# Transposes of the identity in four places of TensorE's queue, and 128 rows instead of 113 in the first product

## The chip, the core and the metric

The kernel runs on one core of a Trainium2 chip. Its engines are TensorE (PE, with its weight loads shown apart as PEld), VectorE (DVE), ScalarE (ACT), GpSimd (POOL) and SyncE (SP, which issues most DMAs). The metric is the device time of one execution in microseconds (us).

## The reference

An agent attention (49 agents between 12480 queries and keys of 128 channels) feeds two expert layers, one after the other:

```
scale = 1 / sqrt(128)
sm(a, b) = softmax(scale * a @ b.T)        # row maximum taken off, 1e-9 added to the sum
agent_v  = sm(agents, k) @ v               # 49 x 128
x   = sm(q, agents) @ agent_v              # 12480 x 128
y   = (s * relu(x @ w_in)**2 + b) @ w_out  # 128 -> 2048 -> 128
out = relu(y @ w_in2)**2 @ w_out2          # 128 -> 2048 -> 128
```

Everything comes in and goes out as float32; the weights come as 64-bit floats and are decoded on the chip.

## The kernel before

**Stage 1, to about 84 us: the agents' values.** The keys come in 13 groups of up to 1024 rows. For each group `k_transpose` transposes eight blocks on PE (L401), `k_scores` multiplies them with the agents (L411), ACT copies the scores to `S` (L413), and `k_max` keeps a running maximum on DVE (L417). Then the maximum over all keys goes through PE twice: `mxk` is transposed (`ps_mt`, L442), DVE reduces it and spreads it on a diagonal (`mt`, `dm`), and a product with ones gives it to every partition (`ps_mb`, L450, copied to `mb`). After that `shift(g)` takes `mb` off a group's scores, on DVE for group 0 and on POOL for groups 1 to 12 (L477), and ACT takes the exponential (L478). PE sums the products with the values, 13 groups into one bank `ps_av` (L494; each product is two records in the trace). `colsum` adds eight products into `ps_cs` (L460), four ahead of the transpose of the normalized values `avn` (`ps_avT`, L510) and four behind it. Block 0 of the queries passes through the same queues: `q_transpose(0)` and `(1)` (L141) around `ps_mt`, `q_scores(0)` (`ps_s`, L167) behind `ps_mb`, `q_exp(0)` (L200), `q_norm(0)` (L206 to L214), `q_stack(0)` (`ps_x`, L223).

**The decode of the weights** is woven in: `fill(n)` issues n steps of it, some eight DVE operations per piece of 512 columns (L269 to L285), with a copy on ACT at its end (L287) and one at its start (L267).

**M = agent_v @ w_in** comes in four pieces (`m_piece`, L338): two at the end of stage 1 and two in the first steps of stage 2. `av` holds the agents' values twice, in columns 0 to 48 and 64 to 112, so that a product gives 113 rows (KS): the second copy meets the low halves of the probabilities in `X`. Rows between the two copies are zero.

**Stage 2, 28 blocks of up to 448 queries**, each in 8 steps. A step issues on PE four products `ps_h` of layer 1 (`up1`, L543, M as weights and X moving), six of layer 2 (`up2`, L554) and twelve of the two way-down products (`down`, L565), while ACT and DVE make the squared relu and its two halves (L530, L531, L112, L113). The remaining decode runs in the first steps.

**Order.** The program is written under a manual schedule: every engine takes its instructions in the order of the Python code, PE, DVE, ACT and POOL each from its own queue. Tiles come from pools: `ps_h` has two buffers of two PSUM banks each, which hold the transposed keys in stage 1 and the hidden layer in stage 2.

Of the kernel before, what the change touches and what calls it, by code (L numbers as in the profile page):

```python
# [9 lines left out]
F32 = mybir.dt.float32  # L10
F32R = mybir.dt.float32r
# [5 lines left out]
P = 128  # L17
# [21 lines left out]
def tile_agent_attention_two_moe(  # L39
# [14 lines left out]
    nc = tc.nc  # L54
    _, N, C = q.shape
    NA = agents.shape[1]
    DFF = w_in.shape[1]
# [4 lines left out]
    KS = GAP + NA  # L62
# [23 lines left out]
    const = ctx.enter_context(tc.tile_pool(name="const", bufs=1))  # L86
    qp = ctx.enter_context(tc.tile_pool(name="qp", bufs=2))
    ps_h = ctx.enter_context(tc.tile_pool(name="ps_h", bufs=2, space=bass.MemoryType.PSUM))
# [3 lines left out]
    ident = const.tile([P, P], F32, name="ident")  # L92
    ones = const.tile([P, P], F32, name="ones")
    aT = const.tile([P, GAP], F32, name="aT")
    M = [const.tile([KS, DFF], F32R, name=f"M{x}") for x in "hl"]
    av = [const.tile([P, KS], F32R, name=f"av{x}") for x in "hl"]
    s_sb = const.tile([P, 1], F32, name="s_sb")
    b_sb = const.tile([P, 1], F32, name="b_sb")
    ones_r = const.tile([P, P], F32R, name="ones_r")
# [5 lines left out]
    sTs = [const.tile([KS, 256], F32, name=f"sT{i}") for i in range(2)]  # L105
    aS = const.tile([P, KS], F32R, name="aS")
    halves = (0, slice(0, NA)), (1, slice(GAP, KS))
    Xs = [const.tile([KS, 512], F32R, name=f"X{i}") for i in range(2)]

    def split(dst, src, eng_lo, copy=nc.vector.tensor_copy):  # L110

        copy(dst[0], src)  # L112
        eng_lo.tensor_tensor(out=dst[1], in0=src, in1=dst[0].bitcast(F32), op=ALU.subtract)  # L113


    q_raw, qT, q_sT, q_e, q_st, X = {}, {}, {}, {}, {}, {}
# [17 lines left out]
    def q_transpose(t):  # L134
        _, p, j = blocks[t]
        n = p * j
        raw = q_raw.pop(t)
        if t < DIRECT:
            ps = ps_m.tile([P, 512], F32, tag="m", name="ps_q")
            for i in range(j):  # L140
                nc.tensor.transpose(  # L141
                    out=ps[:, i * p:(i + 1) * p], in_=raw[:p, i * C:(i + 1) * C], identity=ident[:p, :p]
                )
            qT[t] = qp.tile([P, 512], F32, tag="qh", name="qT")
            nc.scalar.copy(qT[t][:, :n], ps[:, :n])
        else:
            hi = qp.tile([P, 512], F32R, tag="qh", name="qh")
            lo = qp.tile([P, 512], F32R, tag="ql", name="ql")
            split((hi[:, :n], lo[:, :n]), raw[:, :n], nc.vector, nc.scalar.copy)
            qT[t] = (hi, lo)  # L150
# [9 lines left out]
    def q_scores(t):  # L160

        _, p, j = blocks[t]
        x = qT.pop(t)
        ps = ps_m.tile([P, 512], F32, tag="m", name="ps_s")
        sc = ps[:p, :j * NA].rearrange("p (j n) -> p j n", n=NA)
        for i in range(j):
            nc.tensor.matmul(out=sc[:, i], lhsT=x[:, i * p:(i + 1) * p], rhs=aT[:, :NA], start=True, stop=True)  # L167
        q_shift(t, sc)
# [28 lines left out]
    def q_exp(t):  # L197
        _, p, j = blocks[t]
        e = q_e[t]
        nc.scalar.activation(e[:p, :j], e[:p, :j], AF.Exp, scale=SCALE)  # L200
# [57 lines left out]
    def w_decode(raw, hi, lo, early):  # L258

        L, H = raw[:, :, 0], raw[:, :, 1]  # L260
        x = dec_p.tile([P, WC], I32, tag="x", name="x")
        li = dec_p.tile([P, WC], I32, tag="li", name="li")
        ex = dec_p.tile([P, WC], I32, tag="ex", name="ex")
        ts, stt = nc.vector.tensor_scalar, nc.vector.scalar_tensor_tensor
        xf = x.bitcast(F32)
        if early:
            nc.scalar.activation(xf, H.bitcast(F32), AF.Abs)  # L267
        else:
            nc.vector.tensor_single_scalar(out=x, in_=H, scalar=0x7FFFFFFF, op=ALU.bitwise_and)  # L269
            yield  # L270
        ts(out=li, in0=H, scalar1=0x1FF, scalar2=15, op0=ALU.bitwise_and, op1=ALU.logical_shift_left)
        yield
        ts(out=xf, in0=xf, scalar1=W_MIN, scalar2=W_MAX, op0=ALU.max, op1=ALU.min)  # L273
        yield
        stt(out=li, in0=L, scalar=17, in1=li, op0=ALU.logical_shift_right, op1=ALU.bitwise_or)  # L275
        yield
        ts(out=x, in0=x, scalar1=4, scalar2=1, op0=ALU.logical_shift_left, op1=ALU.logical_shift_right)
        yield
        stt(out=x, in0=H, scalar=-(2**31), in1=x, op0=ALU.bitwise_and, op1=ALU.bitwise_or)  # L279
        yield  # L280
        ts(out=ex, in0=x, scalar1=2**30, scalar2=-(2**23), op0=ALU.bitwise_xor, op1=ALU.bitwise_and)  # L281
        yield
        ts(out=x, in0=x, scalar1=2**30, scalar2=-(2**12), op0=ALU.bitwise_xor, op1=ALU.bitwise_and)
        yield
        stt(out=lo, in0=li, scalar=2.0**-35, in1=ex.bitcast(F32), op0=ALU.mult, op1=ALU.mult)  # L285
        yield
        nc.scalar.copy(hi, xf)  # L287
# [12 lines left out]
    def next_load():  # L300
        if to_load:
            src, i, pair = to_load.pop(0)
            loaded.append((w_load(src, i), i, pair))

    def fill(n):

        for _ in range(n):
            if len(running) < 2 and loaded and (not running or min(x[1] for x in running) >= 4):
                raw, i, pair = loaded.pop(0)
                left = len(to_load) + len(loaded) + len(running)  # L310
                sl = slice(i * WC, (i + 1) * WC)
                running.append([w_decode(raw, pair[0][:, sl], pair[1][:, sl], left >= NW), 0])
            if not running:
                return
            r = running.pop(0)
            r[1] += 1
            try:
                next(r[0])
                running.append(r)
            except StopIteration:  # L320
                done.append(0)
            for i in range(len(done)):
                done[i] += 1
            if done and done[0] > 3:
                done.pop(0)
                next_load()
# [6 lines left out]
    def m_piece(i):  # L333

        sl = slice(i * WC, (i + 1) * WC)
        ps = ps_m.tile([P, 512], F32, tag="m", name="ps_M")
        for z, (x, w) in enumerate(((av[0], wi[1]), (av[1], wi[0]), (av[0], wi[0]))):
            nc.tensor.matmul(out=ps[:KS], lhsT=x, rhs=w[:, sl], start=(z == 0), stop=(z == 2))  # L338
        split((M[0][:, sl], M[1][:, sl]), ps[:KS], nc.vector, nc.scalar.copy)

    with tc.manual_schedule():

        with tc.tile_pool(name="pre", bufs=1) as pre, tc.tile_pool(name="kp", bufs=2) as kp:
# [42 lines left out]
            ps = ps_m.tile([P, 512], F32, tag="m", name="ps_w")  # L386
            for i in range(16):
                nc.tensor.transpose(out=ps[:, :P], in_=ident, identity=ident)
            ps = ps_m.tile([P, 512], F32, tag="m", name="ps_a")
# [25 lines left out]
            def k_max(g):  # L415
                _, p, j = kblocks[g]
                nc.vector.tensor_tensor(  # L417
                    out=mxa[:p, :j], in0=S[:p, t0[g]:t0[g] + j], in1=(mxa if g > 1 else S)[:p, :j], op=ALU.max
                )

            for g in range(NG + 1):
# [11 lines left out]
                    k_max(g - 2)  # L433
                fill(FILL_K[g])

            k_max(NG - 1)
            mxk = pre.tile([P, NA], F32, name="mxk")
            nc.vector.reduce_max(mxk, mxa.rearrange("p j n -> p n j"), axis=AX.X)
            q_transpose(0)
            fill(FILL_T)  # L440
            ps = ps_m.tile([P, 512], F32, tag="m", name="ps_mt")
            nc.tensor.transpose(out=ps[:NA, :P], in_=mxk, identity=ident)  # L442
            mt = pre.tile([NA, 1], F32, name="mt")
# [2 lines left out]
            nc.vector.tensor_scalar_mul(dm, ident[:NA, :NA], mt)  # L446
            q_transpose(1)
            fill(FILL_T)
            ps = ps_m.tile([P, 512], F32, tag="m", name="ps_mb")
            nc.tensor.matmul(out=ps[:, :NA], lhsT=ones[:NA], rhs=dm, start=True, stop=True)  # L450
            mb = pre.tile([P, 1, NA], F32, name="mb")
# [30 lines left out]
                shift(g)  # L482
            q_scores(0)
            q_exp(0)
            ps_av = ps_y.tile([P, 512], F32, tag="y1", name="ps_av")
            for g, (_, p, j) in enumerate(kblocks):
                if g + 3 < NG:
# [5 lines left out]
                for i in range(j):  # L493
                    nc.tensor.matmul(  # L494
                        out=ps_av[:NA, :C + 1],
                        lhsT=S[:p, t0[g] + i],
                        rhs=vs[g][:p, i],
                        start=(g == 0 and i == 0),
                        stop=(g == NG - 1 and i == j - 1),
# [6 lines left out]
            nc.vector.reciprocal(rs, rs)  # L506
            avn = pre.tile([NA, C], F32, name="avn")
            nc.vector.tensor_scalar_mul(avn, ps_av[:NA, :C], rs)
            ps = ps_m.tile([P, 512], F32, tag="m", name="ps_avT")
            nc.tensor.transpose(out=ps[:, :NA], in_=avn, identity=ident[:NA, :NA])  # L510
            colsum(NW, 2 * NW)
# [2 lines left out]
            for c0 in (0, GAP):  # L514
                nc.vector.tensor_tensor(
                    out=av[1][:, c0:c0 + NA], in0=ps[:, :NA], in1=av[0][:, c0:c0 + NA].bitcast(F32), op=ALU.subtract
# [20 lines left out]
        def up1(t, i):  # L537
            n = blocks[t][1] * blocks[t][2]
            ps = ps_h.tile([P, 2, 512], F32, tag="h", name="ps_h1")
            for c in range(2):  # L540
                sl = slice((2 * i + c) * P, (2 * i + c + 1) * P)
                for z in (1, 0):
                    nc.tensor.matmul(out=ps[:, c, :n], lhsT=M[z][:, sl], rhs=X[t], start=(z == 1), stop=(z == 0))  # L543

# [54 lines left out]
        for st in range(total + L2 + LAG + 3):  # L599
            t, i = divmod(st, NPR)  # L600
# [29 lines left out]
            t, i = divmod(st - L2, NPR)  # L630
            if 0 <= t < NB:
                up2(t, i)
            t, i = divmod(st - LAG, NPR)
# [4 lines left out]
            t, i = divmod(st - L2 - LAG, NPR)  # L638
# [4 lines left out]
            t, i = divmod(st - L2 - LAG - NPR, NPR)  # L643
# [32 lines left out]
```

## Time and profile before

| | |
|---|---|
| median of three runs | 1139.34 us (1139.15 to 1139.51) |
| the profiled execution | 1138.89 us, of which its span is 1136.9 us |
| PE busy | 1113.1 us (98%) |
| DVE, ACT, POOL busy | 979.4, 943.5, 38.3 us |
| mean granted clock of PE | 0.993 |

The span begins with the first instruction that the profiler saw and ends with the last; some 2 us lie around it. Sums below go by the profiled execution. A granted clock of 1.00 is 2.4 GHz and one of 0.50 is 1.2 GHz, the two levels that appear here. A row that says 48.18 1.73 starts at 48.18 us and lasts 1.73 us; durations of pipelined products overlap, so the pace of a series is taken from its length over its count.

### The profile page before, as it was taken

The page shows a single profiled execution, that of the slowest core. Times are in us where ns is not written, and L with a number is a line of the kernel's source. Part 1 is how long each engine was busy: PE and PEld are TensorE (multiplying, and loading weights), DVE is VectorE, ACT ScalarE, POOL GpSimd, SP SyncE. Part 2 cuts the span into 40 slices and gives each one's busy share as a digit, 9 for nine tenths or more (in the row PEclk, how much of TensorE's full clock was granted, in tenths as well). Part 3 has the DMA queues.
Part 4 walks back from the last instruction along what each step waited for, and adds up shares of the span by engine and source line. Part 5 has one row for each costly group of instructions (what it writes and reads, how often), then busy time and mean ns, then how long its engine had stood idle before and what let it go on. Part 6 is the DMA issues. An engine that isn't in the chain of part 4 may idle for free.

```text
span 1136.9 us, 15468 instructions
## 1 busy us (share of the span) xinstructions
PE 1113.1 (98%) x5787; PEld 1026.2 (90%) x5787; DVE 979.4 (86%) x1425; ACT 943.5 (83%) x1183; POOL 38.3 (3%) x45
## 2 busy tenths in 40 slices
PE   8997899999999999999999999999999999999998
PEld 8986799999999999999999999999999999999997
DVE  5889998888888888888888888888888888888875
ACT  4646798888888888888888888888888888888875
POOL 1226100000000000000000000000000000000000
PEclk9899999999999999999999999999999999999999
DMA  8861009999999999999999999999999999800000
GB/s 309 246 200 35 1 1 23 15 15 7 15 15 15 13 10 15 15 15 8 15 15 15 7 15 15 15 15 8 15 15 15 8 15 15 12 1 9 9 10 15
DMA packets 1285730, 34.96 MB, mean 31 GB/s; under 512 B 1255239, under 2 KB 1281752, under 8 KB 1285656
## 3 DMA queue, kind: packets, MB, share of 16 engines
q1 hardware_dynamic: 1285368, 33.98, 116.0%
q8 instruction: 45, 0.74, 0.4%
q14 instruction: 29, 0.24, 0.1%
q10 hardware_dynamic: 288, 0.00, 0.0%
HBM read 27.58 MB, written 6.39 MB: 30 GB/s over the span
## 4 chain that ended last, share of the span: by engine, by line
PE 87%; DVE 6%; ACT 1%; issue 1%; POOL 0%; DVEq 0%; ACTq 0%
PE ps_y L565 45%; PE ps_h L554 24%; PE ps_h L543 15%; PE ps_o L592 1%; PE ps_sT L177 1%; DVE gh L112 1%; DVE gl L113 0%; ACT r L530 0%; DVE x L273 0%; DVE x L279 0%; DVE li L275 0%; PE ps_x L223 0%; POOL gl L113 0%; PE ps_b L192 0%; DVE ex L281 0%
## 5 line engine op out<-in xcount | busy, mean ns | idle before, releaser
L530 ACT ACTIVATE r<-ps_h 128x896 f32<-128x896 f32 (+1 forms) x448 | 408.7, 912 | 109.0 <-PE ps_h L543 77.7
L113 DVE TENSOR_TENSOR gl<-r,gh 128x896 fp32r<-128x896 f32 (+1 forms) x439 | 477.5, 1088 | 15.1
L531 ACT ACTIVATE r<-r 128x896 f32<-128x896 f32 (+1 forms) x448 | 426.6, 952 | 14.3
L112 DVE CAST gh<-r 128x896 fp32r<-128x896 f32 (+1 forms) x448 | 281.1, 628 | 108.8 <-ACT r L531 97.0
L554 PE MATMUL ps_h<-yh,wi2l 128*128 128x448 f32 (+1 forms) x448 | 169.1, 378 | 2.3 <-DVE yh L112 1.6
L565 PE MATMUL ps_y<-gl,woh 128*128 128x448 f32 (+1 forms) x448 | 163.3, 365 | 5.9 <-POOL gl L113 5.3
L543 PE MATMUL ps_h<-X,Ml 113*128 113x448 f32 (+1 forms) x448 | 166.4, 371 | 0.8 <-DVE Ml L113 0.8
L554 PE MATMUL ps_h<-yl,wi2h 128*128 128x448 f32 (+1 forms) x448 | 163.6, 365 | 0.1
L554 PE MATMUL ps_h<-yh,wi2h 128*128 128x448 f32 (+1 forms) x448 | 163.6, 365 | 0.0
L543 PE MATMUL ps_h<-X,Mh 113*128 113x448 f32 (+1 forms) x448 | 163.5, 365 | 0.0
L565 PE MATMUL ps_y<-gh,wol 128*128 128x448 f32 (+1 forms) x448 | 163.3, 364 | 0.0
L565 PE MATMUL ps_y<-gl,wo2h 128*128 128x448 f32 (+1 forms) x448 | 162.4, 362 | 0.6 <-DVE gl L113 0.6
L565 PE MATMUL ps_y<-gh,woh 128*128 128x448 f32 (+1 forms) x448 | 162.6, 363 | 0.0
L565 PE MATMUL ps_y<-gh,wo2l 128*128 128x448 f32 (+1 forms) x448 | 162.4, 362 | 0.0
L565 PE MATMUL ps_y<-gh,wo2h 128*128 128x448 f32 (+1 forms) x448 | 161.8, 361 | 0.0
L565 PEld LDWEIGHTS ps_y<-gl,woh 128*128 128x128 f32 x448 | 84.5, 189 | 13.5 <-POOL gl L113 6.8
L554 PEld LDWEIGHTS ps_h<-yh,wi2l 128*128 128x128 f32 x448 | 84.4, 188 | 9.7 <-issue 1.9
L554 PEld LDWEIGHTS ps_h<-yl,wi2h 128*128 128x128 f32 x448 | 84.9, 190 | 6.9 <-DVE yl L113 0.6
L543 PEld LDWEIGHTS ps_h<-X,Ml 113*128 113x128 f32 x448 | 84.5, 189 | 7.3 <-issue 1.2
L554 PEld LDWEIGHTS ps_h<-yh,wi2h 128*128 128x128 f32 x448 | 84.3, 188 | 7.0
L565 PEld LDWEIGHTS ps_y<-gh,wol 128*128 128x128 f32 x448 | 84.5, 189 | 6.4 <-ACT y L573 0.4
L565 PEld LDWEIGHTS ps_y<-gl,wo2h 128*128 128x128 f32 x448 | 84.1, 188 | 6.7 <-DVE gl L113 1.2
(122 smaller groups left out, 1025.5 us busy)
## 6 DMA issues: line engine op xcount, KB each, us to landing
kraw<-in_k_dram SPq DMA_DIRECT2D x12, 512.0 KB, 7.7
v<-in_v_dram SPq DMA_DIRECT2D x12, 512.0 KB, 7.3
q_raw<-in_q_dram SPq DMA_DIRECT2D x27, 224.0 KB, 36.3
out_dram<-o SPq DMA_DIRECT2D x27, 224.0 KB, 2.8
raw<-in_moe_w_in_dram SPq DMA_DIRECT2D x8, 512.0 KB, 7.0
raw<-in_moe_w_out_dram SPq DMA_DIRECT2D x8, 512.0 KB, 5.4
q_raw<-in_q_dram SPq DMA_DIRECT2D x1, 192.0 KB, 31.7
out_dram<-o SPq DMA_DIRECT2D x1, 192.0 KB, 2.3
```

The lines of the kernel that those rows point to most:

```text
L112: copy(dst[0], src)
L113: eng_lo.tensor_tensor(out=dst[1], in0=src, in1=dst[0].bitcast(F32), op=ALU.subtract)
L177: nc.tensor.matmul(out=ps[:KS, :n], lhsT=aS, rhs=x[z][:, :n], start=(z == 1), stop=(z == 0))
L530: nc.scalar.activation(r[:, :, :n], ps[:, :, :n], AF.Relu)
L531: nc.scalar.activation(r[:, :, :n], r[:, :, :n], AF.Square)
L543: nc.tensor.matmul(out=ps[:, c, :n], lhsT=M[z][:, sl], rhs=X[t], start=(z == 1), stop=(z == 0))
L554: nc.tensor.matmul(out=ps[:, c, :n], lhsT=w[:, sl], rhs=y[:, :n], start=(z == 0), stop=(z == 2))
L565: nc.tensor.matmul(out=py[t][:, :n], lhsT=wz[:, m], rhs=g[:, c, :n], start=(m == 0 and z == 0), stop=(m == NCH - 1 and z == 2),)
L592: nc.tensor.transpose(out=po[:, i], in_=x[:, i * p:(i + 1) * p], identity=ident)
```

## The change

Four calls `keep_clock(n)` put 10, 6, 8 and 8 transposes of the identity (128 by 128) into PE's queue; their result, a new tile of the pool `ps_h`, is read by nothing. `av`, `M` and `X` get 128 partitions or columns in place of 113; what is added is zero, since `av` and `X` are set to zero at the start.

```diff
-    M = [const.tile([KS, DFF], F32R, name=f"M{x}") for x in "hl"]
-    av = [const.tile([P, KS], F32R, name=f"av{x}") for x in "hl"]
+    M = [const.tile([P, DFF], F32R, name=f"M{x}") for x in "hl"]
+    av = [const.tile([P, P], F32R, name=f"av{x}") for x in "hl"]
...
-    Xs = [const.tile([KS, 512], F32R, name=f"X{i}") for i in range(2)]
+    Xs = [const.tile([P, 512], F32R, name=f"X{i}") for i in range(2)]
...
-            nc.tensor.matmul(out=ps[:KS], lhsT=x, rhs=w[:, sl], start=(z == 0), stop=(z == 2))
-        split((M[0][:, sl], M[1][:, sl]), ps[:KS], nc.vector, nc.scalar.copy)
+            nc.tensor.matmul(out=ps, lhsT=x, rhs=w[:, sl], start=(z == 0), stop=(z == 2))
+        split((M[0][:, sl], M[1][:, sl]), ps, nc.vector, nc.scalar.copy)
...
+            def keep_clock(n):
+
+                ps = ps_h.tile([P, 1024], F32, tag="h", name="ps_w")
+                for _ in range(n):
+                    nc.tensor.transpose(out=ps[:, :P], in_=ident, identity=ident)
...
             fill(FILL_T)
+            keep_clock(10)
             ps = ps_m.tile([P, 512], F32, tag="m", name="ps_mt")
...
             fill(FILL_T)
+            keep_clock(6)
             ps = ps_m.tile([P, 512], F32, tag="m", name="ps_mb")
...
             q_exp(0)
+            keep_clock(8)
             ps_av = ps_y.tile([P, 512], F32, tag="y1", name="ps_av")
...
             nc.vector.tensor_scalar_mul(avn, ps_av[:NA, :C], rs)
+            keep_clock(8)
             ps = ps_m.tile([P, 512], F32, tag="m", name="ps_avT")
```

PE's queue around the maximum of the keys, the kernel before against the changed one (`ps_mt` and `ps_mb` carry the maximum, `ps_q` are the queries' transposes, `ps_s` their first scores, `ps_w` the new transposes, of which an xN row holds N):

```order
 L141 MATMUL ps_q<-ident,q_raw 128x112 x4
-L442 MATMUL ps_mt<-ident,mxk 49x128
+L440 MATMUL ps_w<-ident 128x128 x10
+L449 MATMUL ps_mt<-ident,mxk 49x128
 L141 MATMUL ps_q<-ident,q_raw 128x112 x4
-L450 MATMUL ps_mb<-dm,ones 128x49
+L440 MATMUL ps_w<-ident 128x128 x6
+L458 MATMUL ps_mb<-dm,ones 128x49
 L167 MATMUL ps_s<-aT,qT 112x49 x4
+L440 MATMUL ps_w<-ident 128x128 x8
```

Both products of the maximum now stand behind a row of transposes that wait for nothing, and the first product with the values stands behind eight.

PE's queue from the last products with the values to the transpose of the agents' values, in the kernel before:

```order
L494 MATMUL ps_av<-v_114,S 49x129 [waits DMAHW2_49,Activation_49]
L494 MATMUL ps_av<-v_114,S 49x129
L460 MATMUL ps_cs<-woh,ones_r 128x512
L460 MATMUL ps_cs<-wol,ones_r 128x512
...
L460 MATMUL ps_cs<-wol,ones_r 128x512 [waits DVE_49]
L510 MATMUL ps_avT<-ident,avn 128x49 [waits DVE_49,PE_49]
```

and in the changed kernel:

```order
L503 MATMUL ps_av<-v_114,S 49x129 [waits DMAHW2_49,Activation_49]
L503 MATMUL ps_av<-v_114,S 49x129
L468 MATMUL ps_cs<-woh,ones_r 128x512
...
L468 MATMUL ps_cs<-wol,ones_r 128x512 [waits DVE_49]
L440 MATMUL ps_w<-ident 128x128 [waits PE_49]
L440 MATMUL ps_w<-ident 128x128 x7
L520 MATMUL ps_avT<-ident,avn 128x49 [waits DVE_49,PE_49]
```

The eight transposes stand between the fourth product of `ps_cs` and `ps_avT`. On DVE, ACT, POOL and SP no instruction changes its place.

## Rows read from the trace of the kernel before

**Rows 1.** The page: busy time of each engine; the chain that ended last, by engine.

```profile
PE 1113.1 (98%) x5787; PEld 1026.2 (90%) x5787; DVE 979.4 (86%) x1425; ACT 943.5 (83%) x1183; POOL 38.3 (3%) x45
...
PE 87%; DVE 6%; ACT 1%; issue 1%; POOL 0%; DVEq 0%; ACTq 0%
```

**Rows 2.** The chain in order of time: start us, length us, engine, tile, line.

```profile
51.33 0.27 ACT e L200
...
53.70 0.60 DVE li L275
...
77.34 0.35 DVE avn L508
...
77.83 0.23 PE ps_avT L510
78.06 1.14 PE ps_cs L460 x4
...
138.01 1.48 PE ps_h L554 x6
```

**Rows 3.** PE by stretches: from:to, length, busy (instructions), granted clock, DMA share, GB/s.

```profile
44.70:48.10 3.40, 1.61 (x11) 1.00 1.17 321
48.20:54.90 6.70, 6.70 (x33) 0.50 0.09 31
...
65.20:68.60 3.40, 2.45 (x22) 1.00 0.83 260
...
116.40:119.80 3.40, 1.68 (x8) 1.00 0.00 0
119.90:123.20 3.30, 3.30 (x10) 0.50 0.00 0
...
138.00:1137.00 999.00, 993.62 (x5036) 1.00 1.26 13
```

**Rows 4.** Instructions in order of time, 44 to 51 us: start, length, engine.

```profile
44.91 0.39 PEld L141 LDWEIGHTS ps_q<-ident,q_raw 112*128 112x128 f32 x4 [0.37 <-ACT S L413]
...
46.85 0.28 PE L442 MATMUL ps_mt<-ident,mxk 128*49 128x128 f32 x1 [1.34 <-DVE mxk L438]
46.95 0.39 PEld L141 LDWEIGHTS ps_q<-ident,q_raw 112*128 112x128 f32 x4
...
47.79 0.29 PEld L450 LDWEIGHTS ps_mb<-dm,ones 49*128 49x128 f32 x2 [0.45 <-DVE dm L446]
...
48.18 1.73 PE L167 MATMUL ps_s<-aT,qT 128*112 128x49 f32 x8
...
49.83 7.99 PE L494 MATMUL ps_av<-v,S 128*49 128x129 f32 x48
...
50.80 0.53 ACT L478 ACTIVATE S<-S 128x392 f32<-128x392 f32 x1 [0.37 <-POOL S L477]
```

**Rows 5.** The same view elsewhere: eight transposes early, eight later, eight score records.

```profile
14.88 1.91 PE L401 MATMUL ps_k<-ident,kraw 128*128 128x128 f32 x8
...
39.52 0.92 PEld L401 LDWEIGHTS ps_k<-ident,kraw 128*128 128x128 f32 x8
...
82.88 0.96 PEld L167 LDWEIGHTS ps_s<-aT,qT 128*112 128x112 f32 x8
```

**Rows 6.** The same view, 60 to 76 us: exponentials, products with the values, column sums.

```profile
60.98 0.62 ACT L287 CAST woh<-x 128x512 fp32r<-128x512 f32 x1 [6.83 <-DVE x L283]
...
68.14 7.73 PE L494 MATMUL ps_av<-v,S 128*49 128x129 f32 x68 [0.95 <-ACT S L478]
...
75.80 0.19 PEld L460 LDWEIGHTS ps_cs<-woh,ones_r 128*128 128x128 f32 x1 [0.19 <-issue]
```

**Rows 7.** The page's groups: busy us, mean ns of one, idle before.

```profile
L554 PE MATMUL ps_h<-yh,wi2l 128*128 128x448 f32 (+1 forms) x448 | 169.1, 378 | 2.3 <-DVE yh L112 1.6
L565 PE MATMUL ps_y<-gl,woh 128*128 128x448 f32 (+1 forms) x448 | 163.3, 365 | 5.9 <-POOL gl L113 5.3
L543 PE MATMUL ps_h<-X,Ml 113*128 113x448 f32 (+1 forms) x448 | 166.4, 371 | 0.8 <-DVE Ml L113 0.8
```

## The prediction

> **What bounds the kernel now.** Read the busy times and the chain's shares first: PE is busy 98% of the span and makes 87% of the chain, DVE 6% [rows 1]. That sounds as if any microsecond saved on PE counted, so the second view is the chain in order of time, to see where the shares lie. From 138.01 us on it is PE alone, and the stretch from there to the end has PE busy for 993.62 of 999.00 us [rows 2, 3]. Before that it is mostly DVE: it passes from the exponential of the first queries (51.33) to DVE, stays there from 53.70 until the normalized values `avn` end at 77.69 (77.34 + 0.35), goes over PE for the transpose of the values and the column sums, and then again mostly over DVE and ACT until 138 [rows 2]. So PE's work on the values, 49.83 to 75.80, is not in the chain at all.
>
> The third view is PE by stretches. Its clock is granted at 0.50 from 48.2 to 54.9, after a stretch (44.7 to 48.1) in which it was busy 1.61 of 3.40 us; it is busy throughout at the low level [rows 3]. That is what the transposes address. The fourth view, the instructions in order of time, tells what each of them stands in front of.
>
> **The change part by part.** First the price of one transpose. Eight took 0.92 us at 39.52, so 0.115 us each at 2.4 GHz; eight of the same took 1.91 us at 14.88, 0.24 each, twice as much: the pace of 1.2 GHz [rows 5].
>
> The ten ahead of `ps_mt`: the queries' transposes free the weight path at 44.91 + 0.39 = 45.30; ten at 0.115 last until 46.45. `ps_mt` did not start before 46.85, since it waited 1.34 us for DVE's `mxk` [rows 4]. Cost 0, hidden under DVE's reduction. At the low level the ten would take 2.4 us, reach 47.70 and cost 0.85.
>
> The six ahead of `ps_mb`: free at 46.95 + 0.39 = 47.34, six last until 47.34 + 0.69 = 48.03. `ps_mb` started its weights at 47.79, so it comes 0.24 us later [rows 4]. This is on the chain. Behind `ps_mb` wait DVE's copy `mb`, the subtractions on POOL, ACT's exponentials of groups 1 and 2, behind those in ACT's queue the exponential `e` of the first queries, and behind `e` the DVE work that the chain then follows [rows 2, 4]. Cost +0.24.
>
> The eight ahead of the values, and what the clock gives. If it stays at 1.00, the eight score records of `ps_s` take 0.96 us (82.88) instead of 1.73, and they begin at 48.18 + 0.24 = 48.42; with eight transposes at 0.115 the values start at 48.42 + 0.96 + 0.92 = 50.30 rather than at 49.83. One record of the values costs 7.73 / 68 = 0.114 us at full clock [rows 5, 6], so the 48 of groups 0 to 2 end at 50.30 + 5.47 = 55.77 instead of 57.82. PE gains 2.05 us there, and this is the gain that the low clock suggests. It does not last. ACT stands for 6.83 us before 60.98, waiting for DVE's decode, with the later exponentials queued behind; and at 68.14 PE itself had waited 0.95 us for an exponential that came out of this queue [rows 6]. DVE's work does not get shorter, so the last five groups start at 68.14 + 0.24 again, and PE's gain turns into idle time ahead of them: a gain of 0 at 75.80. The earlier end of `ps_s` frees DVE for the queries' maximum, too, but `e` still stands behind the exponential of group 2, which waits for POOL (50.80) [rows 4]. Gain 0.
>
> The eight ahead of `ps_avT`: column sums start at 75.80 and four of them take 1.14 (by the four at 78.06), to 76.94; eight transposes end at 77.86. `ps_avT` started at 77.83 because `avn` ended at 77.69 [rows 2, 6]. Cost about +0.03; without DVE's delay as cover they would cost their full 0.92.
>
> 128 rows in M, av and X. The products stream as many columns as before (512 and 448), so I take 0. The trace has no 128-row form of this line. Its bounds are its neighbours with 128 rows: the first product of a pair takes 371 ns here, 378 in layer 2 and 365 in the way down [rows 7]. Over 448 of them that is (378 - 371) x 448 = +3.1 us or (365 - 371) x 448 = -2.7 us. The 113-row value lies between two 128-row ones, so rows do not seem to be what tells them apart, and 0 is the middle.
>
> Sum: 0.24 + 0.03 = +0.27 on the profiled execution's 1138.89, 1139.16. The median of the runs lies 0.45 above this execution, so the forecast is 1139.34 + 0.27 = **1139.6 us**.
>
> A rule of the Trainium skill speaks against the purpose. In the trace eight transposes at 14.88 still ran at the low pace, although PE had begun on such work long before [rows 5]. "TensorE: Matmul & The Clock Gate", part 4, says that the full clock does not engage for transposes, since they do not count as activity in the same way. By that rule the clock falls near 48 us all the same. The trace agrees with it so far as it goes; no row shows a clock that transposes alone held or failed to hold. What the sum then would be is the second rival.
>
> **The rivals.**
>
> 1. The low clock comes later instead (slower). By the numbers above PE, now early, ends group 5 near 61.7 and group 7 near 66.5 and stands still for 1.9 us before 68.38, against 0.95 before. With 0.95 idle in 65.2 to 68.6 the clock held, but after 116.4 to 119.8 with 1.72 us idle it fell to 0.50 [rows 3, 6]. A fall at 68 to 72 would halve the pace of the last groups. Low stretches here last 3.3 or 6.7 us [rows 3], so 1.65 or 3.35 us are lost, and since column sums and eight transposes now fill all the time until `avn`, PE has no slack left: 1141.3 or 1143.0. It decides (over 0.2%) once more than 2.0 us are lost, a low stretch above 4 us. For it: idle time of that length was followed by the low clock twice (1.79 us of 44.7 to 48.1 as well). Against: the longer low stretch was seen only behind the thin score products.
>
> 2. The transposes do not hold the clock, so the change does not do what it says. Scores and eight transposes at the low pace then put the values' start at 48.42 + 1.73 + 1.91 = 52.06, 2.23 later. Half of this returns: until 54.9 only 2.84 / 0.228 = 12 records run at half pace instead of 22, so PE is 2.23 - 10 x 0.114 = 1.1 us late from there to 68.14. It had 0.95 us to spare there, and the exponentials are themselves 0.24 late. 1139.6, as the forecast, only by another way.
>
> 3. The score product was in the way after all. `ps_s` would take 0.96 instead of 1.73; were it what DVE's chain starts from, 0.77 would come off: 1139.34 + 0.27 - 0.77 = 1138.8. Against it stands ACT's order [rows 4].
>
> 4. Rows do matter: 1139.6 - 2.7 = 1136.9, or 1139.6 + 3.1 = 1142.7. Nothing but the spread of neighbours speaks for it.
>
> **How the numbers follow.** A measurement of this kernel can tell about 0.2%, 2.28 us, from no change, so "the same" is 1137.06 to 1141.62. Chances: forecast 0.52, rival 1 0.27 (a third of it with the longer stretch), rival 2 0.12, rival 3 0.04, rival 4 0.05, split evenly. Slower is 0.09 from rival 1 and 0.02 from rival 4, 0.11. Faster is 0.02 from rival 4 and 0.01 for what I have overlooked, 0.03. The same is 0.86. The range reaches over rival 3 with room for the scatter of the runs (below 0.2 either way), and some for what no row shows, and over the short form of rival 1 into part of the long one: 1138.1 to 1142.0.
>
> **What would show it.** In the changed profile: PE's clock 1.00 from 48 to 55 (right) or 0.50 (rival 2); `ps_mt` unmoved and `ps_mb` 0.2 to 0.3 us late against `mxk`; the first 48 records of the values done near 55.8, and then two idle gaps of PE that end with ACT's exponentials; DVE without a gap from 53.9 to 77.9; the products with M at 371 and 365 ns. A clock of 0.50 between 68 and 76 is rival 1. The prediction is wrong if the way from `ps_mb` to the end of `avn` becomes shorter than the 29.9 us from 47.79 to 77.69, or if the steady pace after 138 us moves.

## The result and the profile after

The changed kernel takes 1149.66 us (median of six runs, 1148.47 to 1151.33) against 1139.42 of the kernel before on the same chips; the ratio is 1.0084, 95% interval 1.0068 to 1.01. The forecast was 1139.6.

The page of the changed kernel, the lines that answer to [rows 1] and [rows 7]:

```profile
PE 1123.9 (98%) x5819; PEld 1025.4 (89%) x5819; DVE 980.6 (85%) x1425; ACT 943.5 (82%) x1183; POOL 38.4 (3%) x45
...
PE 88%; DVE 4%; ACT 1%; issue 1%; POOL 0%; DVEq 0%; ACTq 0%
...
L564 PE MATMUL ps_h<-yh,wi2l 128*128 128x448 f32 (+1 forms) x448 | 168.1, 375 | 3.5 <-ACT r L540 1.9
L575 PE MATMUL ps_y<-gl,woh 128*128 128x448 f32 (+1 forms) x448 | 164.6, 367 | 5.7 <-POOL gl L113 5.1
L553 PE MATMUL ps_h<-X,Ml 128*128 128x448 f32 (+1 forms) x448 | 166.1, 371 | 0.8 <-DVE Ml L113 0.8
```

No group stands out. The product whose rows were changed (L553) takes 371 ns as before; the way-down products (L575) went from 365 to 367, and PE still waits for next to nothing. So the loss is not a wait. Next, PE by stretches in the changed kernel (columns as in [rows 3]):

```profile
44.00:48.10 4.10, 3.99 (x38) 1.00 1.12 314
48.20:54.90 6.70, 6.42 (x55) 1.00 0.61 177
...
300.00:1100.00 800.00, 800.00 (x3996) 1.00 1.34 12
```

and the last of these for the kernel before:

```profile
300.00:1100.00 800.00, 800.00 (x4043) 1.00 1.32 12
```

The clock is held where it had fallen to 0.50 [rows 3]: the transposes do what they were put there for. But in the 800 us of the steady part PE, busy all the time at the same clock, gets through 3996 records instead of 4043, 1.2% fewer. The chain in order of time shows where. The changed kernel:

```profile
643.62 2.40 PE ps_y L575 x12
646.02 0.81 PE ps_h L553 x4
646.84 1.23 PE ps_h L564 x6
648.06 2.47 PE ps_y L575 x12
```

and the kernel before, at the same place and, first, in an early block:

```profile
149.55 2.47 PE ps_y L565 x12
...
642.62 0.82 PE ps_h L543 x4
643.44 1.23 PE ps_h L554 x6
644.66 2.40 PE ps_y L565 x12
```

Twelve way-down products, with the same shapes, tiles and code, take 2.47 us instead of 2.40: 206 ns from one start to the next instead of 200. Both kernels know both paces. The kernel before has the slower one in its early blocks (2.47 at 149.55) and hardly ever from the sixth block on; the changed one has it in most runs of twelve to the end, with the faster one between (2.40 at 643.62). Counted by their starts from 350 to 1090 us, 3 of 157 runs of twelve are slow in the kernel before and 127 of 158 in the changed one. A list of waits does not show this, and a table of mean durations hardly; starts do.

The profiled execution is the slowest of the six, 1151.33 us. Of the 12.4 us between the two profiled spans, 8.7 lie behind the first product with M, 0.35 in the delay of `ps_mb`, and 3.3 ahead of anything that was changed: in this execution eight transposes at 20.52 us still ran at the low pace, where the kernel before had left it by 18.73. Up to there PE's queue is the same in both, so I do not count this to the change.

```profile
20.52 1.91 PE L401 MATMUL ps_k<-ident,kraw 128*128 128x128 f32 x8
```

### The profile page after: what moved, and what is told of

The parts are those of the page before. It is cut to its first block, busy times and chain, and to the rows that moved or that the text cites. A ratio compares the mean times of both kernels' runs of the same rounds, so it can differ in the third digit from the quotient of the medians.

```text
span 1149.3 us, 15532 instructions
## 1 busy us (share of the span) xinstructions
PE 1123.9 (98%) x5819; PEld 1025.4 (89%) x5819; DVE 980.6 (85%) x1425; ACT 943.5 (82%) x1183; POOL 38.4 (3%) x45
## 4 chain that ended last, share of the span: by engine, by line
PE 88%; DVE 4%; ACT 1%; issue 1%; POOL 0%; DVEq 0%; ACTq 0%
PE ps_y L575 46%; PE ps_h L564 23%; PE ps_h L553 15%; PE ps_o L602 1%; PE ps_sT L177 1%; DVE gh L112 1%; PE ps_av L503 1%; ACT r L540 1%; POOL gl L113 0%; DVE gl L113 0%; PE ps_x L223 0%; ACT r L541 0%; PE ps_b L192 0%; DVE x L273 0%; DVE x L279 0%
## 5 line engine op out<-in xcount | busy, mean ns | idle before, releaser
L575 PE MATMUL ps_y<-gl,woh 128*128 128x448 f32 (+1 forms) x448 | 164.6, 367 | 5.7 <-POOL gl L113 5.1
L553 PE MATMUL ps_h<-X,Ml 128*128 128x448 f32 (+1 forms) x448 | 166.1, 371 | 0.8 <-DVE Ml L113 0.8
L575 PE MATMUL ps_y<-gl,wo2h 128*128 128x448 f32 (+1 forms) x448 | 163.8, 366 | 0.6 <-DVE gl L113 0.6
L575 PE MATMUL ps_y<-gh,wol 128*128 128x448 f32 (+1 forms) x448 | 164.2, 367 | 0.0
L575 PE MATMUL ps_y<-gh,woh 128*128 128x448 f32 (+1 forms) x448 | 164.0, 366 | 0.0
L575 PE MATMUL ps_y<-gh,wo2l 128*128 128x448 f32 (+1 forms) x448 | 163.8, 366 | 0.0
L553 PE MATMUL ps_h<-X,Mh 128*128 128x448 f32 (+1 forms) x448 | 163.2, 364 | 0.0
L575 PE MATMUL ps_y<-gh,wo2h 128*128 128x448 f32 (+1 forms) x448 | 162.4, 362 | 0.0
L575 PEld LDWEIGHTS ps_y<-gl,woh 128*128 128x128 f32 x448 | 84.1, 188 | 15.3 <-POOL gl L113 6.6
L553 PEld LDWEIGHTS ps_h<-X,Ml 128*128 128x128 f32 x448 | 84.4, 188 | 8.7 <-issue 1.2
L575 PEld LDWEIGHTS ps_y<-gl,wo2h 128*128 128x128 f32 x448 | 83.9, 187 | 8.8 <-DVE gl L113 1.2
L575 PEld LDWEIGHTS ps_y<-gh,wol 128*128 128x128 f32 x448 | 84.0, 188 | 8.2 <-ACT y L583 0.4
L575 PEld LDWEIGHTS ps_y<-gh,wo2l 128*128 128x128 f32 x448 | 83.9, 187 | 8.1 <-ACT oT L594 0.3
L575 PEld LDWEIGHTS ps_y<-gh,woh 128*128 128x128 f32 x448 | 84.2, 188 | 7.7
```

The lines of the kernel that those rows point to most:

```text
L575: nc.tensor.matmul(out=py[t][:, :n], lhsT=wz[:, m], rhs=g[:, c, :n], start=(m == 0 and z == 0), stop=(m == NCH - 1 and z == 2),)
```

## Experiments

**What the rows move.** `av` is two tiles of 113 columns, 452 bytes per partition; with 128 columns they are 512. The addresses fit tiles that stand one behind the other, each rounded up to a multiple of 32 bytes, so each of the two grows from 480 to 512. In the built programs the tiles behind them stand at these addresses (bytes in a partition):

```
          before   changed
M high     17792     17792
av low     34656     34688
wo high    35744     35808
wi2 high   52128     52192
X 0        89472     89536
g high 1  175168    175232
```

Everything behind `av` is 64 bytes further, M is not. In the table, M / W / D is how far M, the decoded weights (wo, wi2, wo2) and the data tiles behind them (X, y, g) stand from their old place; "records" are PE's in 300 to 1100 us; the pace is the mean from start to start of way-down products that follow one another between 350 and 1090 us, worked out from each trace. It is a mean: in most of these kernels each run of twelve is either at 200 or at 206, and the mean tells how many are slow.

| kernel | M / W / D | rows | transposes | median us | ratio (95%) | records | pace ns |
|---|---|---|---|---|---|---|---|
| before | 0 / 0 / 0 | 113 | no | 1139.42 | | 4043 | 199.9 |
| transposes alone (e1) | 0 / 0 / 0 | 113 | yes | 1140.30 | 1.0008 (0.9998 to 1.0019) | 4042 | 199.9 |
| change, old addresses (e4) | 0 / 0 / 0 | 128 | yes | 1139.68 | 0.9989 (0.9979 to 0.9999) | 4039 | 200.7 |
| all moved with M (g1) | 64 / 64 / 64 | 128 | yes | 1142.45 | 1.0021 (1.0005 to 1.0037) | 4029 | 201.3 |
| W and D by 128 (f3) | 0 / 128 / 128 | 128 | yes | 1142.99 | 1.0018 (1.0008 to 1.0028) | 4030 | 201.5 |
| weights at 128 (g4) | 0 / 96 / 128 | 113 | no | 1141.27 | 1.0014 (1.0 to 1.0028) | 4029 | 201.7 |
| 64 bytes alone (e3) | 0 / 64 / 64 | 113 | no | 1144.07 | 1.0037 (1.0022 to 1.0052) | 4018 | 203.1 |
| weights moved (f1) | 0 / 64 / 128 | 128 | yes | 1147.07 | 1.0057 (1.0038 to 1.0075) | 4005 | 204.0 |
| data moved (f2) | 0 / 0 / 64 | 128 | yes | 1149.49 | 1.0074 (1.0056 to 1.0093) | 4003 | 204.5 |
| rows alone (e2) | 0 / 64 / 64 | 128 | no | 1148.94 | 1.0071 (1.0048 to 1.0094) | 3999 | 205.1 |
| the changed kernel | 0 / 64 / 64 | 128 | yes | 1149.66 | 1.0084 (1.0068 to 1.01) | 3996 | 205.3 |
| M by 64, W and D by 128 (f4) | 64 / 128 / 128 | 128 | yes | 1149.29 | 1.0078 (1.0062 to 1.0094) | 3992 | 205.7 |

Executions of the kernel before lie between 1137.1 and 1142.6 us, so medians differ by a microsecond or two for nothing; pace and records are the sharper measures.

**First four: which part of the change.** The transposes alone (M, av and X back at 113 rows):

```diff
-    av = [const.tile([P, P], F32R, name=f"av{x}") for x in "hl"]
+    av = [const.tile([P, KS], F32R, name=f"av{x}") for x in "hl"]
```

> The changed kernel with its four rows of transposes, but with M, av and X at 113 rows as before, so that every later tile stands at its old address. Addresses theory (av wider by 60 bytes each pushes every tile behind it by 64 bytes per partition, and the way-down products then keep 205 ns instead of 200): 1139.6 us, way-down pace 200 ns. Rows theory (a product with 128 contracting rows slows the ones beside it): the same 1139.6. Phase theory (the transposes shift the engines against each other at the start, and the later rhythm locks another way): 1149 us, pace 205 ns.

The rows alone (all four calls taken out):

```diff
-            keep_clock(10)
...
-            keep_clock(8)
```

> M, av and X at 128 rows, no transposes. Addresses theory: 1149 us, way-down pace 205 ns. Rows theory: 1149 us, 205 ns. Phase theory: 1139.3 us, 200 ns.

The kernel before with an unused tile:

```diff
+    pad = const.tile([P, 16], F32, name="pad")
     s_sb = const.tile([P, 1], F32, name="s_sb")
```

> The kernel before with nothing changed but an unused tile of 64 bytes per partition behind av, so that all tiles behind it stand at the addresses of the changed kernel. Addresses theory: 1149 us, way-down pace 205 ns. Rows theory and phase theory: 1139.4 us, 200 ns.

The whole change at the old addresses:

```diff
-    s_sb = const.tile([P, 1], F32, name="s_sb")
-    b_sb = const.tile([P, 1], F32, name="b_sb")
     ones_r = const.tile([P, P], F32R, name="ones_r")
-    y1_bias = const.tile([P, 1], F32, name="y1_bias")
+    sby = const.tile([P, 3], F32, name="sby")
+    s_sb, b_sb, y1_bias = (sby[:, i:i + 1] for i in range(3))
```

> The whole change, but the three one-column tiles s_sb, b_sb and y1_bias share one tile, which gives the 64 bytes back: all tiles from ones_r on stand at the addresses of the kernel before. Addresses theory: 1139.6 us, way-down pace 200 ns. Rows theory and phase theory: 1149 us, 205 ns.

The transposes alone keep the old pace and cannot be told from no change; the phase theory falls. The whole change at the old addresses is as fast as before, which the rows theory excludes. An unused tile of 64 bytes in the kernel before costs 0.37%. So the moved addresses are a cause by themselves, and without them there is no loss to be seen. But the addresses theory wanted 1149 us and 205 ns of the unused tile, and it gave 1144.07 and 203.1, about half the loss. The other half needs both: at the moved addresses 128 rows run at 205.1 ns and 113 rows at 203.1, at the old ones 200.7 and 199.9. How the rows add to it is not shown. PE in 300 to 1100 us, the unused tile alone:

```profile
300.00:1100.00 800.00, 800.00 (x4018) 1.00 1.33 12
```

and the whole change at the old addresses:

```profile
300.00:1100.00 800.00, 800.00 (x4039) 1.00 1.33 12
```

What 203.1 is made of, the chain shows. These are the eight runs of twelve of one block with the unused tile alone:

```profile
642.59 2.48 PE ps_y L566 x12
...
647.11 2.40 PE ps_y L566 x12
...
651.57 2.48 PE ps_y L566 x12
...
656.73 2.47 PE ps_y L566 x12
...
661.23 2.40 PE ps_y L566 x12
...
665.68 2.48 PE ps_y L566 x12
...
670.63 2.40 PE ps_y L566 x12
...
675.27 2.40 PE ps_y L566 x12
```

Four are slow and four fast, and it is the same four in nearly every block from 300 us on. In the whole change at the old addresses it is mostly one of eight, in the changed kernel six, at times seven. The halves that these products stream stand in three buffers by turns, and eight is not a multiple of three, so the buffer is not what picks the slow steps.

**Second four: whose place counts.** All four are the changed kernel with 64 unused bytes in one of three places: behind the weights (f1, and f2, which has `sby` as above too), ahead of them (f3), or ahead of M (f4):

```diff
+    pad = const.tile([P, 16], F32, name="pad")
     stacks = [const.tile([P, 4, GAP], F32, name=f"stack{i}") for i in range(2)]
...
+    pad = const.tile([P, 16], F32, name="pad")
     wo = [const.tile([P, NCH, C], F32R, name=f"wo{x}") for x in "hl"]
...
+    pad = const.tile([P, 16], F32, name="pad")
     M = [const.tile([P, DFF], F32R, name=f"M{x}") for x in "hl"]
```

> The changed kernel with 64 unused bytes behind the weights: the decoded weights of the two layers (wo, wi2, wo2) stay 64 bytes off their old place, all tiles behind them (X, the hidden halves g, y, the raw and decoded pieces) stand 128 bytes off it. If a place counts only by its remainder to 128 bytes, the weights are moved and the rest is not. Weights theory (the place of the weights sets the pace of the way-down products): 1149 us, 206 ns. Data theory (the place of the moving tiles, which ACT and DVE write and PE streams, sets it): 1139.7 us, 200 ns. Distance theory (the distance to M, which stands ahead of all of them and never moved, sets it): between, since weights are 64 and data 128 off.

> The whole change with the weights at their old place (the three one-column tiles in one, as in the run before), and 64 unused bytes behind the weights, so that the data tiles alone stand 64 bytes off. Weights theory: 1139.7 us, way-down pace 200 ns. Data theory: 1149 us, 206 ns. Distance theory: between.

> The changed kernel with 64 more unused bytes ahead of the weights: weights and data stand 128 bytes off their old place. If the remainder to 128 bytes counts, by any of the three theories: 1139.7 us, 200 ns. If any move from the old place is as bad, or a longer period counts: about 1149 us, 206 ns.

> The changed kernel with 64 unused bytes ahead of M: weights and data stand 128 bytes off their old place, M 64. Weights and data theories, M left out of them: 1139.7 us, way-down pace 200 ns. Distance theory: as the changed kernel, 1149 us, 206 ns, since all distances are those of the changed kernel.

In f1 and f2, with weights and data 64 bytes out of step, the pace is 204.0 and 204.5: neither theory by itself, which both wanted one of the two at 200. No run of twelve is at 200 or at 206 throughout there; in f2 every third product is followed after 200 or 201 ns and most others after 205 to 207. Moving both by 128 returns most of the pace (201.5). f3 and f4 have weights and data in the same place and differ in M (and the small tiles between), and f4 is as slow as the changed kernel, whose distances it has. The way-down products do not read M; the four products of layer 1 between two runs of twelve do. That speaks for the distances between the tiles.

**Third four: distances, and whose pace it is.** In g1, M, weights and data all move by 64 (`sby`, and the unused tile ahead of M):

> The whole change with the one-column tiles in one (which takes 64 bytes away) and 64 unused bytes ahead of M: M, the weights and the data all stand 64 bytes off their old place, so every distance among them is the old one, and the weights and the data stand where the slow changed kernel has them. Distance theory: 1139.7 us, way-down pace near 200 ns. Place theory (the place of the weights or the data by itself): 1149 us, 205 ns.

The weights and data stand exactly where the slow kernel has them, and the pace is 201.3. The distance theory holds for the larger part. Its chain in order of time has both paces:

```profile
613.51 2.41 PE ps_y L575 x12
618.61 2.47 PE ps_y L575 x12
```

The two quiet kernels leave out the squared relu and its two halves on ACT and DVE from block 8 on; the way-down products read an older step's halves:

```diff
-        def hidden(ps, n, layer, eng_lo=nc.vector):
+        def hidden(ps, n, layer, eng_lo=nc.vector, old=False):
+            if old:
+                last[layer].append(last[layer][-3])
+                return last[layer][-1]
...
-            G2[t, i] = hidden(ps, n, 2)
+            G2[t, i] = hidden(ps, n, 2, old=t >= 8)
```

> The changed kernel, which from block 8 on leaves out the squared relu and its halves on ACT and DVE: the way-down products read the halves of an older step again, at the same addresses, and PE runs almost alone. If the pace of the way-down products is PE's own, set by the addresses that it reads one after the other: 205 ns there, as with all engines. If ACT's and DVE's accesses to the same memory make it: below that, the same as in its twin with the old addresses.

> The twin of the run before with the old addresses (one-column tiles in one), from block 8 on without the squared relu and its halves. PE's own pace: 200 ns in the way-down products. Other engines' accesses: equal to its twin.

All engines in 300 to 1100 us (PE, PEld, DVE, ACT, POOL busy, then clock and DMA), the quiet kernel with the changed addresses:

```profile
300.00:1100.00 800.00, 800.00 (x4008) 733.47 (x4008) 188.49 (x378) 147.71 (x250) 0.00 (x0) 1.00 1.33 12
```

and with the old ones:

```profile
300.00:1100.00 800.00, 800.00 (x4054) 742.68 (x4053) 187.89 (x377) 146.23 (x247) 0.00 (x0) 1.00 1.33 12
```

DVE is busy for 188 us and ACT for 148, against 695 and 694 in the changed kernel, and PE's difference stays, 4008 records against 4054 and 204.8 ns against 200.5. The medians are 1146.42 (ratio 1.0061, 1.0038 to 1.0084) and 1136.40 (0.9964, 0.9949 to 0.998), 10 us apart as with all engines. So ACT's and DVE's work on the halves does not make the slower pace.

Last, the weights at multiples of 128 bytes, from the kernel before (unused tiles of 96 and 32 bytes ahead of and behind the weights):

> The kernel before with the weights 96 and the data 128 bytes further, so that the weights begin at multiples of 128 bytes, as M does, instead of 32 behind one. Distance theory: the distances of the weights to M and to the data change by a quarter of 128 bytes, so the pace may land at either of the two values or between them: 199 to 206 ns, 1139 to 1149 us. Place theory with whole lines: at or below 1139.3 us.

In the steady part every run of twelve takes 2.43 us, between the two:

```profile
613.05 2.43 PE ps_y L567 x12
618.15 2.43 PE ps_y L567 x12
```

It is a mixture and not a third pace. By the starts in the trace every third product, the high half on the high weights, is followed after 206 or 207 ns, and the other two after 199 to 201:

```profile
612.89 0.36 PE L567 MATMUL ps_y<-gh,wol 128*128 128x448 f32 x1
613.09 0.36 PE L567 MATMUL ps_y<-gl,woh 128*128 128x448 f32 x1
613.29 0.37 PE L567 MATMUL ps_y<-gh,woh 128*128 128x448 f32 x1
613.50 0.36 PE L567 MATMUL ps_y<-gh,wol 128*128 128x448 f32 x1
```

No version beats the kernel before in pace. The whole change at the old addresses has a ratio just below 1, but with a pace of 200.7 against 199.9 nothing in its steady part is faster; I count it as equal.

## Why the prediction was wrong, and where it was right

**The step that failed** is "128 rows in M, av and X. The products stream as many columns as before (512 and 448), so I take 0." It looked at the shape of the products that were changed and not at the memory behind them: 15 more columns in `av` push every later tile by 64 bytes, which alone brings the way-down products from 199.9 to 203.1 ns, and 128 rows at the moved places bring them to 205.1. Its bounds, -2.7 to +3.1 us, were drawn for 448 products of layer 1 and could not hold an effect that sits in the 2688 way-down products, which the change does not touch. In the steady part each is, in the mean, 5.4 ns slower (205.3 - 199.9), 0.52 us per block of 96; other products give 0.11 of it back, by the starts of the steps. The kernel before ran its first blocks partly at the slow pace, which leaves 8.7 us in all. The prediction also said what would refute it, "if the steady pace after 138 us moves", and that is what moved. A sign was there: the same twelve products at 2.47 and 2.40 us in one trace, read past because the mean durations agree.

**The transposes** went as forecast. The kernel with them alone, in order of time:

```profile
45.86 1.26 PE L440 MATMUL ps_w<-ident 128*128 128x128 f32 x10
47.39 0.28 PE L449 MATMUL ps_mt<-ident,mxk 128*49 128x128 f32 x1 [0.27 <-DVE mxk L444]
...
47.92 0.82 PE L440 MATMUL ps_w<-ident 128*128 128x128 f32 x6
48.67 0.42 PE L458 MATMUL ps_mb<-dm,ones 49*128 49x49 f32 x2
...
50.83 5.52 PE L503 MATMUL ps_av<-v,S 128*49 128x129 f32 x48
...
63.54 3.74 PE L503 MATMUL ps_av<-v,S 128*49 128x129 f32 x32 [1.37 <-ACT S L486]
69.03 7.73 PE L503 MATMUL ps_av<-v,S 128*49 128x129 f32 x68 [1.74 <-ACT S L486]
...
78.72 0.23 PE L520 MATMUL ps_avT<-ident,avn 49*128 49x49 f32 x1
```

and two of its weight loads:

```profile
47.83 0.68 PEld L440 LDWEIGHTS ps_w<-ident 128*128 128x128 f32 x6
48.67 0.29 PEld L458 LDWEIGHTS ps_mb<-dm,ones 49*128 49x128 f32 x2 [0.17 <-DVE x L283]
```

- Ten ahead of `ps_mt`: hidden, it still waits for `mxk`. Right.
- Six ahead of `ps_mb`: 1.28 us lie between the starts of `ps_mt` and `ps_mb`, before 0.94 [rows 4]. +0.34, forecast +0.24. The price of the six was right: their weight loads take 0.68 us, 0.113 each. But the sum let `ps_mb` load at once behind them, at 47.83 + 0.68 = 48.51, and it loads at 48.67. What fills these 0.16 us is not shown; the direction and the path were right, the size a little small.
- Eight ahead of the values: the 48 records take 5.52 us (forecast 5.47) instead of 7.99, and the gain then turns into two waits for exponentials, 1.37 and 1.74 us (the second forecast as 1.9). From `ps_mb` to `ps_avT` 30.05 us pass, before 30.04 [rows 2, 4]: a gain of nothing, as said.
- Eight ahead of `ps_avT`: no cost to be seen in that same sum. Right.
- The transposes hold the clock. In the stretch in which it was 0.50 [rows 3], the kernel with them alone has:

```profile
48.20:54.90 6.70, 6.70 (x60) 1.00 0.20 63
61.00:68.50 7.50, 4.91 (x43) 1.00 0.81 240
68.50:76.00 7.50, 6.97 (x63) 1.00 0.64 189
```

Every one of the traces with the transposes shows 1.00 from 48.2 to 54.9; those without show 0.50, 0.54, 0.75 and 0.50. So rival 2 falls, and with it, for this kernel, the rule that stood beside it ("TensorE: Matmul & The Clock Gate", part 4, in the Trainium skill): here transposes kept the clock up. Rival 1 falls too: 1.37 and 1.74 us of waiting lie in 61.0 to 69.0 and the clock stays at 1.00.
- Rival 3: `ps_s` ended earlier, 1.34 us behind the start of `ps_mb` (49.02 + 0.99 - 48.67) where it was 2.12 before [rows 4], and nothing came of it by `ps_avT`. Rival 4 named the right edit, the rows, with the wrong mechanism and a third of the size; it got a chance of 0.05.

**What stays open.** Equal distances restore most of the pace, not all: 201.3 and 201.5 ns against 200.7, 2 us or so of time. Which of the distances (M to X, weights to the halves) does what was not separated. Nor is it shown why 128 rows add to the loss at the moved addresses, what picks the slow steps of a block, or how PE comes to pass from one pace to the other.

## What to carry to other kernels

A change of a tile's size moves every tile allocated behind it; before a kernel that is bound by one engine is credited or blamed for an edit, compare its addresses with the old ones, or give the bytes back. When the bound engine is busy all the time and no wait has grown, count its instructions in a fixed stretch, or measure from start to start; mean durations of pipelined products hide a 3% change. And work that is sped up off the chain turns into a wait: the place to look for it is ahead of the next instruction that stands behind another engine.

## What the runs showed of the hardware

A way-down product with 448 columns at the full clock starts some 200 or some 206 ns after the last. In most of these kernels a run of twelve is at one or the other throughout, and how many runs are slow depends on where tiles lie in the memory, down to 64 bytes: 3 of 157 in the kernel before, 79 of 157 with an unused tile of 64 bytes (e3), 127 of 158 in the changed kernel. It goes with the distances among the tiles more than with their places: moving M along brings the pace from 205.3 to 201.3 ns (g1). With the weights 96 and the data 128 bytes further every third product is slow, and each run takes 2.43 us. With DVE and ACT mostly silent (188 and 148 us busy of 800) the difference stays, 204.8 against 200.5 ns, so it is not contention with their work on the halves. The products with 113 and with 128 rows take the same 371 ns, but the rows do shift which pace is met (203.1 against 205.1 ns at the same addresses).
